# Attention, routing and experts in one kernel on one core: one straight code for every chunk of tokens, each with a rider of up to 32 tokens, in place of four code variants per chunk

## The chip, the cores and the metric

The kernel runs on 1 core of one Trainium2 chip. The metric is the device time of one execution in microseconds (us). Engines are named as in the profile: PE is TensorE (PEld its weight loads), DVE VectorE, ACT ScalarE, POOL GpSimd, SP SyncE.

## The reference

Eight batches of attention between 512 positions and 32 state rows, 8 heads of 64, give 8 x 544 = 4352 rows of 512 numbers. Rows with a positive skip score then go through one of eight experts, chosen by a gate; all others are returned as they are.

```python
def _attn_ref(x, state):                 # x [8,8,512,64], state [8,8,32,64]
    a = softmax(scale * x @ state^T);   xread = a @ state
    a2 = softmax(scale * state @ x^T);  sread = a2 @ x
    return concatenate([xread, sread], axis=2)

def _moe_ref(x, w_skip, w_gate, w1, w2): # x [4352, 512], E = 8, F = 1024
    out = x.copy()
    xc = x[x @ w_skip > 0]
    e_idx, gate_w = argmax and its softmax value of xc @ w_gate
    for e in range(8):
        y[e_idx == e] = gate_w * (relu(xc[e_idx == e] @ w1[e]) @ w2[e])
    out[x @ w_skip > 0] = xc + y
```

(Shortened: the softmax is written out in the original, and the sums are spelled in numpy.)

With the inputs used here the experts 0 to 7 get 544, 0, 0, 32, 544, 1024, 512 and 64 tokens.

## The kernel before

**First phase.** Attention is computed batch by batch and its rows are written to `out` in DRAM. Each batch's rows are scored; the numbers of the rows that an expert has to compute are written into that expert's list `lst` in DRAM by indirect DMAs. When most batches are through, the first full chunk (512 tokens of one expert, chunk 0, here of expert 5) starts beside the rest of it.

**Chunks.** `big(c)` computes one chunk of up to `CB` = 512 tokens of one expert. The numbers of its rows come from `lst` (`lfetch`, `lids`), the rows are gathered from `out` by POOL's indirect DMAs (`zgather`, 16 of 32 rows each), turned and split into a high and a low part (`zsplit`). Weights come in eight pieces of w1 and w2 (`wload`, two DMAs of 256 KB each, issued by SP) and are split by ACT and DVE (`wsplit`). Each product is three matmuls (lines 678 to 680). ACT and DVE make the hidden layer's two halves (L1253, L1254). At the chunk's end DVE adds the result to the rows (L1111) and POOL scatters them back to `out` (L1104). The next chunk's list, rows and weights are fetched while the current chunk computes. Each chunk has a written order per engine (`manual_schedule`), so each engine runs the instructions of a chunk, its own and the next one's loads, in the order in which they stand.

**Riders.** An expert's tokens beyond its full chunks, below 385 of them, are computed in single fp32 matmuls by `rider`, whose steps are strewn between the matmuls of a chunk: four list loads (L1144), the row numbers `rid` (L1151), a gather `rx` (L1153), transposes (L1160), the layers `ph` (L1170) and `yr` (L1183), the sum (L1187) and a scatter. With up to 32 tokens the 128 rows of TensorE hold four quarters of the columns, with up to 64 two halves, with up to 128 one piece. The rider's weights `rw` (4 MB) are loaded in the chunk before it (`rload1`, `rload2`).

**What decides the code.** `chunk_list` computes on DVE, from the counts, a small table `ti`: which chunks and which riders there are, their experts and rows. Each engine reads it into registers (`number`, L285). Chunk c, from 1 to 11, exists four times: with a rider of 32, without one, with one of 128 and with one of 64 (`full`, lines 1291 to 1297). The last chunk that there is, the one behind which no other has to be loaded, runs another set of these four, which stands in the `Else` of the chunk (L1306) behind the code of all later chunks. Riders left when the chunks are through are done in `tails` (L1320).

With these inputs chunk 0 is followed by chunks 1 to 4 (experts 0, 4, 5 and 6). The riders in them are the 32 tokens of expert 0, the 32 of expert 3, the 32 of expert 4 and the 64 of expert 7, this last in chunk 4; `tails` has nothing to do.

Of the kernel before, what the change touches and what calls it, by code (L numbers as in the profile page):

```python
# [32 lines left out]
NBIG = NT // BIGMIN  # L33
NSLOT = 3 * E
# [170 lines left out]
def kernel(ctx, tc, x, state, w_skip, w_gate, w1, w2, out, nb=B):  # L205
# [64 lines left out]
    sizeb = const.tile([P, 3, NSLOT], F32, name="sizeb")  # L270


    ti = const.tile([P, 8], I32, name="ti")
# [16 lines left out]
    def lfetch(c):  # L290

        row = number(c - 1, 5 if c else 1, E * STRIDE - WIN, SP)
        nc.sync.dma_start(out=lis[c % 4][:],
                          in_=lst[ds(row, WIN), :].rearrange("(t p) c -> p t c", p=P))
        size = sizeb[:, 0, c - 1:c] if c else size0[:, 0:1]
# [59 lines left out]
    def expert(c):  # L355
        return number(c - 1, 2 if c else 0, E - 1, SP)
# [133 lines left out]
    thr2 = iota("thr2", [P, E, 3], [[0, E], [P, 3]], 0, 0)  # L490
    slotc = iota("slotc", [P, 1], [[0, 1]], 0, 1)
    slotn = iota("slotn", [P, 1], [[0, 1]], 1, 1)
    stsl = const.tile([P, 3], F32, name="stsl")
    for i, n in enumerate((CB, P, P)):
        G.iota(stsl[:, i:i + 1], pattern=[[0, 1]], base=0, channel_multiplier=n,
               allow_small_or_imprecise_dtypes=True)
    stepn = const.tile([P, 3], F32, name="stepn")
    G.memset(stepn[:], float(P))
    G.memset(stepn[:, 0:1], float(CB))
    cls = const.tile([P, 3], F32, name="cls")  # L500
    for i, n in enumerate((0.0, 32.0, 64.0)):
        G.memset(cls[:, i:i + 1], n)
# [46 lines left out]
    def chunk_list():  # L549
        w = lambda n, s: wk.tile(s, F32, name=n)  # L550
        two = lambda a: a[:].unsqueeze(1).to_broadcast([P, 2, E])
        t8 = w("t8", [P, E, 8])
        nv = w("nv", [P, 3, E])
# [6 lines left out]
        V.tensor_reduce(out=nv[:, 0], in_=t8, axis=AX.X, op=ALU.add)  # L560
        yield
        eb = w("eb", [P, E])
        V.scalar_tensor_tensor(out=eb, in0=nv[:, 0], scalar=float(CB), in1=cw,
# [24 lines left out]
        end = w("end", [P, 1])  # L588
        V.tensor_scalar(out=end, in0=slotn, scalar1=cum[:, 0, E - 1:E], scalar2=4.0,
                        op0=ALU.is_equal, op1=ALU.mult)  # L590
        yield
        ohv = w("ohv", [P, 3, E])
        V.tensor_tensor(out=ohv, in0=ge[:, :, 0:E], in1=ge[:, :, 1:E + 1], op=ALU.subtract)
        yield
        V.tensor_tensor(out=par[:, 2, 0], in0=eb, in1=eu, op=ALU.add)
        yield
        V.tensor_tensor(out=par[:, 2, 1:3], in0=two(cw), in1=two(eu), op=ALU.add)
# [18 lines left out]
        size = w("size", [P, 3])  # L616
# [4 lines left out]
        c3 = w("c3", [P, 3, 3])  # L621
        V.tensor_tensor(out=c3, in0=size[:].unsqueeze(2).to_broadcast([P, 3, 3]),
                        in1=cls[:].unsqueeze(1).to_broadcast([P, 3, 3]), op=ALU.is_gt)
        yield
        kc = w("kc", [P, 3])
        V.tensor_reduce(out=kc, in_=c3, axis=AX.X, op=ALU.add)
        yield
        V.scalar_tensor_tensor(out=kc[:, 0:1], in0=kc[:, 1:2], scalar=1.0, in1=tv[:, 3, 0:1],
                               op0=ALU.add, op1=ALU.mult)
        yield  # L630
        V.tensor_tensor(out=ti[:, 0:1], in0=kc[:, 0:1], in1=end, op=ALU.add)
        yield
        V.tensor_copy(ti[:, 1:2], kc[:, 2:3])
        yield
        V.tensor_copy(ti[:, 2:8].rearrange("p (k a) -> p k a", k=2), tv[:, 0:2, :])
        yield
        dg = w("dg", [P, 3, NSLOT])
        V.tensor_tensor(out=dg, in0=ident[:, 0:NSLOT].unsqueeze(1).to_broadcast([P, 3, NSLOT]),
                        in1=size[:].unsqueeze(2).to_broadcast([P, 3, NSLOT]), op=ALU.mult)
        yield 6  # L640
        psz = ps["t"]([P, 3 * NSLOT], "psz")
        T.matmul(psz, ones[:], dg[:], start=True, stop=True)
        yield 1
        V.tensor_copy(sizeb[:].rearrange("p a n -> p (a n)"), psz)
        yield

    def rest():
# [22 lines left out]
        for f in range(8):  # L670
# [3 lines left out]
            if f == 5:  # L674
                rload(rexpert(0))
# [440 lines left out]
    def rexpert(r, tail=False):  # L1116
        return number(r, 4 if tail else 3, E - 1, SP)
# [18 lines left out]
    def rider(M, r, tail=False):  # L1136
# [4 lines left out]
        row = number(r, 7 if tail else 6, E * STRIDE - P, SP)  # L1141
# [4 lines left out]
        V.tensor_scalar(out=ov, in0=tok[M], scalar1=sizeb[:, 2 if tail else 1, r:r + 1],  # L1146
# [44 lines left out]
    def big(c, M=None, more=True):  # L1191

        xH, xL = xHs[c % 2], xLs[c % 2]
        ride = rider(M, c - 1) if M else iter(())
# [20 lines left out]
        else:  # L1215
# [66 lines left out]
    def kind(c):  # L1282
        return number(c - 1, 0, 8, mybir.ALL_ENGINES)

    def full(c, kd, more):

        def variant(M=None):
            with tc.manual_schedule(engines=order):
                big(c, M, more)

        with tc.If(kd < 3) as cmp2:
            with tc.If(kd > 1) as cmp3:
                variant(32)
            with cmp3.Else():
                variant()
        with cmp2.Else():
            with tc.If(kd > 3) as cmp3:  # L1297
                variant(P)
            with cmp3.Else():
                variant(64)  # L1300

    def chunk(c, kd):
        if c == NBIG:
            full(c, kd - 4, False)
            return
        with tc.If(kd < 5) as cmp:  # L1306
# [6 lines left out]
    def tail_class(r):  # L1313
        return number(r, 1, 3, mybir.ALL_ENGINES) if r < NSLOT else None

    def tails(r, kd):

        if r == NSLOT:
            return
        with tc.If(kd > 0):  # L1320
            kn = tail_class(r + 1)
            if r:
                rload(rexpert(r, tail=True))
            with tc.If(kd > 1) as cmp:
                with tc.If(kd > 2) as cmp2:
                    for _ in rider(P, r, tail=True):
                        pass
                with cmp2.Else():
                    for _ in rider(64, r, tail=True):
                        pass  # L1330
            with cmp.Else():
                for _ in rider(32, r, tail=True):
                    pass
            tails(r + 1, kn)
# [5 lines left out]
    kt = tail_class(0)  # L1340
    kd = kind(1)
    with tc.If(kd > 0):
        chunk(1, kd)
    tails(0, kt)
# [25 lines left out]
```

## Time and profile before

| | us |
|---|---|
| runs | 424.32, 427.35, 429.0 |
| median | 427.35 |
| the profiled execution | 421.62 |
| its span in the trace | 419.3 |
| PE busy | 355.9 (85% of the span) |
| PE idle ahead of a chunk's first matmul (L678, `ph`) | 29.3, of which 28.2 put down to `issue` |
| chunks 1 to 4 on PE | 172.81 to 406.08 |

Times inside the trace count from the span's start. `issue` is time in which an engine waited for nothing that the profile shows. A row's `COMPARE_BRANCH` is the instruction of an engine's sequencer that decides on a jump; these are not counted as busy.

### The profile page before, as it was taken

The page shows a single profiled execution, that of the slowest core. Times are in us where ns is not written, and L with a number is a line of the kernel's source. Part 1 is how long each engine was busy: PE and PEld are TensorE (multiplying, and loading weights), DVE is VectorE, ACT ScalarE, POOL GpSimd, SP SyncE. Part 2 cuts the span into 40 slices and gives each one's busy share as a digit, 9 for nine tenths or more (in the row PEclk, how much of TensorE's full clock was granted, in tenths as well). Part 3 has the DMA queues.
Part 4 walks back from the last instruction along what each step waited for, and adds up shares of the span by engine and source line. Part 5 has one row for each costly group of instructions (what it writes and reads, how often), then busy time and mean ns, then how long its engine had stood idle before and what let it go on. Part 6 is the DMA issues. An engine that isn't in the chain of part 4 may idle for free. (4 is left out here: it accounts for less than half of the span.)

```text
span 419.3 us, 7772 instructions
## 1 busy us (share of the span) xinstructions
PE 355.9 (85%) x2675; PEld 281.0 (67%) x2675; DVE 224.8 (54%) x437; ACT 153.8 (37%) x279; POOL 195.4 (47%) x232
## 2 busy tenths in 40 slices
PE   7699897988789959999996999969999405999960
PEld 7577676876668848887784877758878304876750
DVE  1599998999768623644464435463364700433130
ACT  3589775775562223223231232313233200232000
POOL 8357497687385460427713377231774400310030
PEclk9789997989899988999998999989999955999995
DMA  7916975865694069975598443994539930125621
GB/s 223 182 27 171 303 206 166 214 128 175 193 352 126 1 131 356 389 233 152 167 315 293 111 152 114 367 369 115 146 103 302 370 115 8 42 72 202 213 84 35
DMA packets 77075, 77.81 MB, mean 186 GB/s; under 512 B 30608, under 2 KB 59280, under 8 KB 75952
## 3 DMA queue, kind: packets, MB, share of 16 engines
q1 hardware_dynamic: 70320, 62.25, 48.8%
q0 software_dynamic: 6112, 14.32, 10.6%
q8 instruction: 36, 0.59, 0.7%
q14 instruction: 63, 0.52, 0.5%
q10 hardware_dynamic: 544, 0.13, 0.1%
HBM read 60.95 MB, written 14.83 MB: 181 GB/s over the span
## 5 line engine op out<-in xcount | busy, mean ns | idle before, releaser
L678 PE MATMUL ph<-xH,wH 128*128 128x512 f32 x160 | 68.0, 425 | 29.3 <-issue 28.2
L1253 ACT ACTIVATE hH<-ph 128x512 fp32r<-128x512 f32 x40 | 23.9, 598 | 139.6 <-PE ph L680 135.9
L1254 DVE SCALAR_TENSOR_TENSOR hL<-ph,hH 128x512 fp32r<-128x512 f32 x40 | 27.6, 691 | 72.0 <-ACT hH L1253 72.0
L680 PE MATMUL ph<-xH,wL 128*128 128x512 f32 x160 | 65.2, 407 | 0.5 <-DVE wL L382 0.5
L679 PE MATMUL ph<-xL,wH 128*128 128x512 f32 x160 | 65.3, 408 | 0.0
L678 PE MATMUL y<-wH,hH 128*128 128x512 f32 x160 | 63.5, 397 | 0.0
L679 PE MATMUL y<-wL,hH 128*128 128x512 f32 x160 | 62.6, 391 | 0.0
L680 PE MATMUL y<-wH,hL 128*128 128x512 f32 x160 | 62.6, 391 | 0.0
L678 PEld LDWEIGHTS ph<-xH,wH 128*128 128x128 f32 x160 | 31.8, 199 | 38.4 <-issue 30.3
L343 POOL DMA_INDIRECT z<-out_dram,zi x48 | 50.2, 1045 | 14.6 <-issue 14.6
L382 DVE TENSOR_TENSOR wL<-raw,wH 128x1024 fp32r<-128x1024 f32 x40 | 48.9, 1223 | 8.4 <-ACT wH L379 8.1
L411 POOL DMA_INDIRECT lst<-pays,si x34 | 36.0, 1058 | 19.1 <-issue 7.2
L379 ACT CAST wH<-raw 128x1024 fp32r<-128x1024 f32 x40 | 41.7, 1042 | 6.5 <-PE y L680 4.2
L1104 POOL DMA_INDIRECT out_dram<-xg,sid x20 | 20.8, 1038 | 36.0 <-DVE xg L1111 32.4
L680 PEld LDWEIGHTS ph<-xH,wL 128*128 128x128 f32 x160 | 31.6, 198 | 8.4 <-DVE wL L382 1.0
L678 PEld LDWEIGHTS y<-wH,hH 128*128 128x128 f32 x160 | 30.1, 188 | 9.2 <-issue 3.0
L679 PEld LDWEIGHTS ph<-xL,wH 128*128 128x128 f32 x160 | 31.9, 199 | 6.2
L680 PEld LDWEIGHTS y<-wH,hL 128*128 128x128 f32 x160 | 30.0, 188 | 6.6
L679 PEld LDWEIGHTS y<-wL,hH 128*128 128x128 f32 x160 | 30.1, 188 | 6.2
L1153 POOL DMA_INDIRECT rx<-out_dram,rid x4 | 5.0, 1244 | 55.2 <-DVE rid L1151 36.3
L318 POOL DMA_INDIRECT xg<-out_dram,sid x20 | 20.9, 1046 | 13.8 <-issue 11.3
L1104 POOL DMA_INDIRECT out_dram<-rx,rid x4 | 4.8, 1188 | 48.1 <-DVE rx L1187 25.7
(195 smaller groups left out, 604.5 us busy)
## 6 DMA issues: line engine op xcount, KB each, us to landing
raw<-in_moe_w_dram SPq DMA_DIRECT2D x80, 256.0 KB
rw<-in_moe_w_dram SPq DMA_DIRECT2D x40, 512.0 KB
out_dram<-xr SPq DMA_DIRECT2D x8, 1024.0 KB
xt<-in_x_dram SPq DMA_DIRECT2D x6, 1024.0 KB
xt<-in_x_dram SPq DMA_DIRECT2D x4, 256.0 KB
xt<-in_x_dram SPq DMA_DIRECT2D x2, 512.0 KB
z<-out_dram,zi POOLq DMA_INDIRECT x48, 3.0
sd<-in_state_dram SPq DMA_DIRECT2D x10, 64.0 KB
```

Source lines behind the costliest of these rows:

```text
L318: G.indirect_dma_start(xgs[c % 2][:, t, :], None, out[0:rows, :], bass.IndirectOffsetOnAxis(ap=sis[c % 4][:, t:t + 1], axis=0), bounds_che ...
L343: G.indirect_dma_start(z[:, g], None, rows, bass.IndirectOffsetOnAxis(ap=zis[c % 2][:, g:g + 1], axis=0), bounds_check=4 * NT - 1, oob_is_ ...
L379: A.copy(h, raw)
L382: V.tensor_tensor(out=l, in0=raw, in1=h[:].bitcast(F32), op=ALU.subtract)
L411: d = G.indirect_dma_start(lst[:], bass.IndirectOffsetOnAxis(ap=si[:, j:j + 1], axis=0), pay[:, j, :], None, bounds_check=E * STRIDE - 1, ...
L678: T.matmul(ps, lh, rh, start=first, stop=False)
L679: T.matmul(ps, lh, rl, start=False, stop=False)
L680: T.matmul(ps, ll, rh, start=False, stop=last)
L1104: d = G.indirect_dma_start(rows, bass.IndirectOffsetOnAxis(ap=ids, axis=0), src, None, bounds_check=rows.shape[0] - 1, oob_is_err=False)
L1153: G.indirect_dma_start(rx[:, 0:n2], None, rows, bass.IndirectOffsetOnAxis(ap=ids[:, 0:1], axis=0), bounds_check=NT * Q - 1, oob_is_err=False)
L1253: A.activation(hH, ph, AF.Relu)
L1254: V.scalar_tensor_tensor(out=hL, in0=ph, scalar=0.0, in1=hH[:].bitcast(F32), op0=ALU.max, op1=ALU.subtract)
```

## The change

The classes of riders become lists of fixed sizes: CHUNKS of 512, SMALLS of up to 32, LARGES of up to 128, and LEFT, the smalls for which there is no chunk. An expert's remainder of up to 64 becomes one or two smalls, a larger one becomes larges. Every chunk c from 1 to 11 now has a single code: it always carries rider c - 1 of the smalls (which may be empty) and always loads the rows and weights of chunk c + 1, also where that chunk doesn't exist. Chunks are nested in plain `If`s without `Else`. Behind them the smalls that are left run alone, the first with the weights that the last chunk loaded, others in a loop; then the larges in a loop.

With these inputs the smalls are expert 0, 3, 4 and two halves of expert 7: five. Chunks 1 to 4 carry one each, one is left, and there are no larges.

```diff
     def rexpert / rider: by list (SMALLS, LARGES, LEFT) instead of by class and tail
...
-    def big(c, M=None, more=True):
+    def big(c):
         xH, xL = xHs[c % 2], xLs[c % 2]
-        ride = rider(M, c - 1) if M else iter(())
+        more = c < NBIG
+        ride = rider(SMALLS, c - 1) if c else iter(())
...
-            if M:
-                add(1, 2, go)
-                for i in range(10):
-                    add(3 + i // 2, 2 + 4 * (i % 2), go)
-            if c < NSLOT:
-                er = rexpert(c)
-                add(5 if M == P else 4, 3, rload1, er)
-                add(6 if M == P else 5, 4, rload2, er)
+            add(1, 2, go)
+            for i in range(10):
+                add(3 + i // 2, 2 + 4 * (i % 2), go)
+            er = rexpert(SMALLS, c)
+            add(4, 3, rload1, er)
+            add(5, 4, rload2, er)
...
-    def full(c, kd, more):
-        def variant(M=None):
-            with tc.manual_schedule(engines=order):
-                big(c, M, more)
-        with tc.If(kd < 3) as cmp2:
-            with tc.If(kd > 1) as cmp3:
-                variant(32)
-            with cmp3.Else():
-                variant()
-        with cmp2.Else():
-            with tc.If(kd > 3) as cmp3:
-                variant(P)
-            with cmp3.Else():
-                variant(64)
     def chunk(c, kd):
-        if c == NBIG:
-            full(c, kd - 4, False)
-            return
-        with tc.If(kd < 5) as cmp:
-            kn = kind(c + 1)
-            full(c, kd, True)
-            chunk(c + 1, kn)
-        with cmp.Else():
-            full(c, kd - 4, False)
+        with tc.If(kd > 0):
+            kn = there(c + 1) if c < NBIG else None
+            with tc.manual_schedule(engines=order):
+                big(c)
+            if c < NBIG:
+                chunk(c + 1, kn)
...
+    def alone(which, r, load=True):
+        if load:
+            rload(rexpert(which, r))
+        for _ in rider(which, r):
+            pass
...
-    with tc.If(kd > 0):
-        chunk(1, kd)
-    tails(0, kt)
+    chunk(1, k1)
+    with tc.If(left > 0):
+        alone(LEFT, 0, load=False)
+        with tc.For_i(1, left, 1) as r:
+            alone(LEFT, r)
+    with tc.If(larges > 0):
+        G.memset(rx[:], 0.0)
+        with tc.For_i(0, larges, 1) as r:
+            alone(LARGES, r)
```

In `chunk_list` the tables grow from three lists to four, the steps for the rider classes go and steps for the two kinds of thresholds and for the tables `sizeb` and `tiT` come (33 steps on DVE instead of 32); at the start POOL fills some more constants.

What stands on PE at the end of chunk 1 before the change, where its variant with a rider of 32 ends and the variant without one follows (line 680 is the last matmul of a chunk, `ph<-xH` the first of the next code):

```order
L678 MATMUL y_2160<-wH_2131,hH 128x512
L679 MATMUL y_2160<-wL_2134,hH 128x512
L680 MATMUL y_2160<-wH_2131,hL 128x512
L1292 UNCONDITIONAL_BRANCH
L678 MATMUL ph<-xH_2139,wH_102 128x512
L679 MATMUL ph<-xL_2140,wH_102 128x512
```

Some 600 rows further on, behind all four variants, stands how chunk 2 is entered:

```order
L1297 UNCONDITIONAL_BRANCH
L285 TENSOR_LOAD ti
L1306 COMPARE_AND_BRANCH
L1291 COMPARE_AND_BRANCH
L1292 COMPARE_AND_BRANCH
L678 MATMUL ph<-xH_123,wH_102 128x512
L679 MATMUL ph<-xL_124,wH_102 128x512
```

After the change, the same place on PE, the end of chunk 1 and the start of chunk 2:

```order
L689 MATMUL y_2166<-wH_2137,hH 128x512
L690 MATMUL y_2166<-wL_2140,hH 128x512
L691 MATMUL y_2166<-wH_2137,hL 128x512
L292 TENSOR_LOAD ti
L1305 COMPARE_AND_BRANCH
L689 MATMUL ph<-xH_123,wH_102 128x512
L690 MATMUL ph<-xL_124,wH_102 128x512
```

The jump at the variant's end and the 600 rows between have gone, and of the three branches ahead of chunk 2 one is left.

At the program's end SP has these rows after the change, behind the code of chunk 11 (the branches of L1305 close the chunks; L1163 loads the list of the rider that is left; L1329 is the loop for further ones):

```order
L1305 UNCONDITIONAL_BRANCH x12
L292 TENSOR_LOAD ti
L1327 COMPARE_AND_BRANCH
L292 TENSOR_LOAD ti
L1163 ISA
L1163 DMA rli<-lst 32x2
L1163 ISA
L1163 DMA rli<-lst 32x2
L1163 ISA
L1163 DMA rli<-lst 32x2
```

And PE has these at the same place:

```order
L1305 UNCONDITIONAL_BRANCH x12
L292 TENSOR_LOAD ti
L1327 COMPARE_AND_BRANCH
L1179 MATMUL pt<-ident,rx 128x128
L1189 MATMUL ph<-rw_2147,rxT 32x256 x16
L1196 MATMUL pt<-ident,rh 128x128 x2
L1202 MATMUL yr<-rw_2148,rhT 32x128 x32
L1329 COMPARE_AND_BRANCH
```

With these inputs PE and SP come here from the end of chunk 4, over the code of chunks 5 to 11, and the rider that rode in chunk 4 as a form of 64 is, for its second half, done here.

More of the change, by code (lines that the diff above doesn't have):

```diff
@@ L33 @@
 NBIG = NT // BIGMIN
+SMALL = 32
+NSMALL = 2 * E
 NSLOT = 3 * E
@@ L269 @@
     size0 = const.tile([P, 1], F32, name="size0")
-    sizeb = const.tile([P, 3, NSLOT], F32, name="sizeb")
-    ti = const.tile([P, 8], I32, name="ti")
+    CHUNKS, SMALLS, LARGES, LEFT = range(4)
+    sizeb = const.tile([P, 8, NSLOT], F32, name="sizeb")
+    tiT = const.tile([1, 4, NSLOT], I32, name="tiT")
+    ti = const.tile([P, 11], I32, name="ti")
+    EXPERT, ROW = 3, 7
     ti0 = const.tile([1, 2], I32, name="ti0")
@@ L355, in expert @@
     def expert(c):
-        return number(c - 1, 2 if c else 0, E - 1, SP)
+        return number(c - 1, EXPERT + CHUNKS if c else 0, E - 1, SP)
     def wload(c, e, f0, f1):
@@ L489 @@
     thr = iota("thr", [P, E, 8], [[0, E], [CB, 8]], BIGMIN, 0)
[L490 removed]
+    thr2 = const.tile([P, 2, E, 3], F32, name="thr2")
+    sgn2 = const.tile([P, 2, E, 3], F32, name="sgn2")
+    G.memset(sgn2[:], 1.0)
+    G.memset(sgn2[:, 0, :, 2], -2.0)
+    for i, n in enumerate((0, SMALL, 2 * SMALL)):
+        G.memset(thr2[:, 0, :, i], float(n))
+    for i, n in enumerate((2 * SMALL, P, 2 * P)):
+        G.memset(thr2[:, 1, :, i], float(n))
     slotc = iota("slotc", [P, 1], [[0, 1]], 0, 1)
[L492 to L494 removed]
+    steps = (CB, SMALL, P, SMALL)
+    stsl = const.tile([P, 4], F32, name="stsl")
+    stepn = const.tile([P, 4], F32, name="stepn")
+    for i, n in enumerate(steps):
         G.iota(stsl[:, i:i + 1], pattern=[[0, 1]], base=0, channel_multiplier=n,
                allow_small_or_imprecise_dtypes=True)
[L497 to L502, printed above, removed]
+        G.memset(stepn[:, i:i + 1], float(n))
     le = const.tile([P, E, E], F32, name="le")
@@ L549, in chunk_list @@
     def chunk_list():
[L550 to L553, printed above, removed]
+        w = lambda n, s, tag=None: wk.tile(s, F32, name=n, **(dict(tag=tag) if tag else {}))
+        many = lambda a, n: a[:].unsqueeze(1).to_broadcast([P, n, E])
+        t8 = w("t8", [P, E, 8], "t64")
+        nv = w("nv", [P, 4, E])
         cw = w("cw", [P, E])
@@ L559, in chunk_list @@
         yield
-        V.tensor_reduce(out=nv[:, 0], in_=t8, axis=AX.X, op=ALU.add)
+        V.tensor_reduce(out=nv[:, CHUNKS], in_=t8, axis=AX.X, op=ALU.add)
         yield
         eb = w("eb", [P, E])
-        V.scalar_tensor_tensor(out=eb, in0=nv[:, 0], scalar=float(CB), in1=cw,
+        V.scalar_tensor_tensor(out=eb, in0=nv[:, CHUNKS], scalar=float(CB), in1=cw,
                                op0=ALU.mult, op1=ALU.min)
@@ L587, in chunk_list @@
         yield
-        end = w("end", [P, 1])
-        V.tensor_scalar(out=end, in0=slotn, scalar1=cum[:, 0, E - 1:E], scalar2=4.0,
-                        op0=ALU.is_equal, op1=ALU.mult)
+        V.tensor_scalar(out=ti[:, LARGES - 1:LEFT], in0=cum[:, LARGES:LEFT + 1, E - 1], scalar1=0.0,
+                        scalar2=None, op0=ALU.max)
         yield
-        ohv = w("ohv", [P, 3, E])
+        ohv = w("ohv", [P, 4, E])
         V.tensor_tensor(out=ohv, in0=ge[:, :, 0:E], in1=ge[:, :, 1:E + 1], op=ALU.subtract)
         yield
-        V.tensor_tensor(out=par[:, 2, 0], in0=eb, in1=eu, op=ALU.add)
+        V.tensor_tensor(out=par[:, 2, CHUNKS], in0=eb, in1=eu, op=ALU.add)
         yield
-        V.tensor_tensor(out=par[:, 2, 1:3], in0=two(cw), in1=two(eu), op=ALU.add)
+        V.tensor_tensor(out=par[:, 2, 1:4], in0=many(cw, 3), in1=many(eu, 3), op=ALU.add)
         yield
@@ L620, in chunk_list @@
         yield
-        c3 = w("c3", [P, 3, 3])
-        V.tensor_tensor(out=c3, in0=size[:].unsqueeze(2).to_broadcast([P, 3, 3]),
-                        in1=cls[:].unsqueeze(1).to_broadcast([P, 3, 3]), op=ALU.is_gt)
+        V.tensor_copy(ti[:, CHUNKS:CHUNKS + 1], tv[:, 3, CHUNKS:CHUNKS + 1])
         yield
-        kc = w("kc", [P, 3])
-        V.tensor_reduce(out=kc, in_=c3, axis=AX.X, op=ALU.add)
+        V.tensor_copy(ti[:, EXPERT:].rearrange("p (k a) -> p k a", k=2), tv[:, 0:2, :])
         yield
-        V.scalar_tensor_tensor(out=kc[:, 0:1], in0=kc[:, 1:2], scalar=1.0, in1=tv[:, 3, 0:1],
-                               op0=ALU.add, op1=ALU.mult)
+        dg = w("dg", [P, 8, NSLOT], "t192")
+        diag = lambda out, a, n: V.tensor_tensor(
+            out=out, in0=ident[:, 0:NSLOT].unsqueeze(1).to_broadcast([P, n, NSLOT]),
+            in1=a.unsqueeze(2).to_broadcast([P, n, NSLOT]), op=ALU.mult)
+        diag(dg[:, 0:4], size[:], 4)
         yield
-        V.tensor_tensor(out=ti[:, 0:1], in0=kc[:, 0:1], in1=end, op=ALU.add)
+        diag(dg[:, 4:6], tv[:, 0, LARGES:LEFT + 1], 2)
         yield
[L633 to L639, printed above, removed]
+        diag(dg[:, 6:8], tv[:, 1, LARGES:LEFT + 1], 2)
         yield 6
-        psz = ps["t"]([P, 3 * NSLOT], "psz")
+        psz = ps["t"]([P, 8 * NSLOT], "psz")
         T.matmul(psz, ones[:], dg[:], start=True, stop=True)
@@ L1113, in finish, with listed, rexpert @@
         scatter(out[:, :], sis[c % 4][:, t:t + 1], xg)
-    def rexpert(r, tail=False):
-        return number(r, 4 if tail else 3, E - 1, SP)
+    def listed(which, r, k, most):
+        if isinstance(r, int):
+            return number(r, (EXPERT, ROW)[k] + which, most, SP)
+        return nc.values_load(tiT[:, 2 * k + which - LARGES, ds(r, 1)], engines=SP, min_val=0,
+                              max_val=most, skip_runtime_bounds_check_because=WHY)
+    def rexpert(which, r):
+        return listed(which, r, 0, E - 1)
     def rload1(e):
@@ L1134, in rload, with rider @@
         rload2(e)
-    def rider(M, r, tail=False):
+    def rider(which, r):
+        M = steps[which]
         Q = P // M
@@ L1140, in rider @@
         rows = out[:, :].rearrange("n (q d) -> (n q) d", q=Q)
-        row = number(r, 7 if tail else 6, E * STRIDE - P, SP)
+        row = listed(which, r, 1, E * STRIDE - P)
         li = small.tile([P, 2], F32, tag="rli", name="rli")
@@ L1145, in rider @@
         ov = small.tile([P, 1], F32, tag="rov", name="rov")
-        V.tensor_scalar(out=ov, in0=tok[M], scalar1=sizeb[:, 2 if tail else 1, r:r + 1],
+        V.tensor_scalar(out=ov, in0=tok[M], scalar1=sizeb[:, which, ds(r, 1)],
                         scalar2=float(4 * OOB), op0=ALU.is_ge, op1=ALU.mult)
@@ L1280, in big, with there, chunk @@
             pass
-    def kind(c):
-        return number(c - 1, 0, 8, mybir.ALL_ENGINES)
-    def full(c, kd, more):
-        def variant(M=None):
-            with tc.manual_schedule(engines=order):
-                big(c, M, more)
-        with tc.If(kd < 3) as cmp2:
-            with tc.If(kd > 1) as cmp3:
-                variant(32)
-            with cmp3.Else():
-                variant()
-        with cmp2.Else():
-            with tc.If(kd > 3) as cmp3:
-                variant(P)
-            with cmp3.Else():
-                variant(64)
-    def chunk(c, kd):
-        if c == NBIG:
-            full(c, kd - 4, False)
-            return
-        with tc.If(kd < 5) as cmp:
-            kn = kind(c + 1)
-            full(c, kd, True)
-            chunk(c + 1, kn)
-        with cmp.Else():
-            full(c, kd - 4, False)
[L1313 to L1334, printed above, removed]
+    def there(c):
+        return number(c - 1, 0, 1, mybir.ALL_ENGINES)
+    def chunk(c, kd):
+        with tc.If(kd > 0):
+            kn = there(c + 1) if c < NBIG else None
+            with tc.manual_schedule(engines=order):
+                big(c)
[6 more added lines that the diff above has]
+            pass
     todo.append(rest())
@@ L1339 @@
     manual.close()
-    kt = tail_class(0)
-    kd = kind(1)
-    with tc.If(kd > 0):
-        chunk(1, kd)
-    tails(0, kt)
+    k1 = there(1)
+    larges = number(0, LARGES - 1, NSLOT, mybir.ALL_ENGINES)
+    left = number(0, LEFT - 1, NSMALL, mybir.ALL_ENGINES)
+    chunk(1, k1)
[7 more added lines that the diff above has]
+            alone(LARGES, r)
 _INS = ["x", "state", "moe_w_skip", "moe_w_gate", "moe_w1", "moe_w2"]
```

51 lines of the change are left out of this document (29 added, 22 removed).

## The prediction

> **What bounds the kernel now.** I cut the end of the profiled execution at the places where TensorE starts and ends a chunk, and read the windows view with the busy time of each engine (the count of its instructions in brackets), the granted TensorE clock, the DMA share and GB/s:
>
> ```profile
> core 0: us, PE busy (x) PEld busy (x) DVE busy (x) ACT busy (x) POOL busy (x), PEclk, DMA share, GB/s
> 172.81:221.48 48.67, 48.67 (x292) 38.44 (x290) 24.76 (x36) 15.58 (x23) 22.95 (x21) 1.00 0.75 240
> 221.48:225.16 3.68, 0.01 (x1) 0.04 (x1) 3.53 (x5) 0.40 (x1) 2.37 (x3) 0.97 1.07 374
> 225.16:275.99 50.83, 50.83 (x291) 39.62 (x291) 23.17 (x34) 15.01 (x22) 24.35 (x24) 0.97 0.62 203
> 275.99:279.60 3.61, 0.01 (x1) 0.03 (x1) 3.57 (x5) 0.41 (x1) 2.25 (x3) 0.99 1.05 367
> 279.60:330.00 50.40, 50.40 (x291) 39.69 (x291) 23.18 (x34) 14.99 (x22) 25.00 (x24) 0.97 0.63 200
> 330.00:350.91 20.91, 0.00 (x1) 0.03 (x1) 3.91 (x7) 0.41 (x1) 4.58 (x5) 0.60 0.47 156
> 350.91:406.08 55.17, 54.78 (x246) 40.75 (x246) 15.44 (x20) 10.46 (x15) 8.56 (x9) 0.97 0.31 107
> 406.08:419.30 13.22, 0.00 (x0) 0.00 (x0) 0.40 (x1) 0.00 (x0) 1.81 (x2) 0.62 0.23 69
> ```
>
> Long rows are chunks 1 to 4, in which TensorE never pauses; short rows are the gaps behind chunks 1, 2 and 3 and the tail of 13.22. Between chunk 0 and chunk 1 there is no gap at all, as the timeline shows (start, duration):
>
> ```profile
> 172.58 0.39 PE L680 MATMUL y<-wH,hL 128*128 128x512 f32 x1
> 172.81 0.39 PE L678 MATMUL ph<-xH,wH 128*128 128x512 f32 x1
> ...
> 225.16 0.77 PE L678 MATMUL ph<-xH,wH 128*128 128x512 f32 x1 [3.68 <-issue]
> ```
>
> So the stretch is bound by TensorE and by whatever holds it at a chunk's edge. The view of waits (us in total, times, longest) gives for that `issue`, nothing that the profile can name:
>
> ```profile
> PE ph L678 <- issue: 28.2, 3, 20.9
> ```
>
> What TensorE's sequencer does there stands in the branch instructions at the edges (duration min/median/max in ns, first and last start):
>
> ```profile
> L1306 PEldq COMPARE_BRANCH  x1: 71/71/71, 169.7 to 169.7; - x1
> ...
> L1292 PEldq COMPARE_BRANCH  x2: 68/3312/6557, 217.5 to 224.9; - x2
> ...
> L1306 PEldq COMPARE_BRANCH  x1: 7835/7835/7835, 333.1 to 333.1; - x1
> ...
> L1291 PEldq COMPARE_BRANCH  x1: 4837/4837/4837, 341.2 to 341.2; - x1
> ```
>
> A branch that falls through takes 0.07 us (into chunk 1, 169.7; 224.9). A taken one takes 4.8 to 7.8. The one at 217.5 ends at 224.06, and 3.9 us of it lie under matmuls still queued; the rest is the gap. Into chunk 4 four are taken one after the other, at lines 1292, 1306, 1291 and 1297, hence 20.91.
>
> **What the change removes.** At the ends of chunks 1, 2, 3 no variant is left to jump over, and chunk 4 is no longer behind in a block of its own; TensorE meets one branch per edge, which falls through as at 169.7. Gaps: 3.68 + 3.61 + 20.91 = **28.2**.
>
> Chunks 2, 3 and 4 begin at half clock:
>
> ```profile
> 225.16:227.20 2.04, 2.04 (x5) 1.67 (x6) 0.00 (x0) 0.00 (x0) 1.67 (x2) 0.50 0.97 339
> ```
>
> That makes 50.83 and 50.40 of chunk 1's 48.67. With no gap the clock stays up: 2.16 + 1.73. Chunk 4 loses its cold start and its rider of 64, becoming chunk 1's form with a rider of 32: 55.17 - 48.67 = 6.50. Together **10.4**. TensorE's last chunk then ends at 172.81 + 4 x 48.67 = 367.5 instead of 406.08.
>
> What covers that: the next chunk's gathers, splits and weights must be in time without the gap. In chunk 1 they were, with DVE at 24.76, POOL at 22.95 and a share of 0.75 after an edge without a gap, so I cost it at nothing. If the cover fails, each edge pays again at most what the queues did in the gap, 3.7 us; three edges, 0 to 11. I take 0, chunk 1 being the same code on the same engines. Chunk 4 newly issues the loads of a chunk 5 that does not exist (eight weight pairs, 16 gathers whose indices are all out of bounds, splits); as in chunk 3 they fit beside TensorE, 23.18 on DVE, 25.00 on POOL.
>
> **What it adds ahead of chunk 1.** One more small DVE step in `chunk_list`, wider tables, some six more fills on POOL at the start. SyncE there waits for something else:
>
> ```profile
> SPq L293 <- DMA lst<-pays,si: 9.5, 2, 7.3
> ```
>
> The list's rows land after the table is made, so nothing to 1 us; I take 0.3. T, the end of chunk 4 on TensorE, is **367.8**.
>
> **What it adds behind.** Five groups of up to 32 tokens for four chunks: expert 7's 64 tokens are two of them, so one rider runs alone after T, with nothing beside it. Its weights are loaded in chunk 4. I walk the chain from T by these rows:
>
> ```profile
> 336.00:338.00 2.00, 0.00 (x0) 0.00 (x0) 0.00 (x0) 0.00 (x0) 0.00 (x0) 0.50 0.98 325
> 338.00:340.00 2.00, 0.00 (x0) 0.00 (x0) 0.00 (x0) 0.00 (x0) 0.00 (x0) 0.50 0.39 112
> ...
> L1306 SPq COMPARE_BRANCH  x1: 50/50/50, 335.2 to 335.2; - x1
> ...
> L1291 SPq ALU_OP  x1: 44/44/44, 341.3 to 341.3; - x1
> L1291 SPq COMPARE_BRANCH  x1: 54/54/54, 341.4 to 341.4; - x1
> ...
> L1297 SPq ALU_OP  x1: 36/36/36, 343.5 to 343.5; - x1
> ...
> 226.63 1.86 SPq L1144 DMA_DIRECT2D rli<-lst  x4
> ...
> 235.83 0.16 DVE L1151 SCALAR_TENSOR_TENSOR rid<-rli,rov 128x1 int32<-128x1 f32 x1
> ...
> 236.90 1.04 POOL L1153 DMA_INDIRECT rx<-out_dram,rid  x1 [9.77 <-DVE rid L1151]
> ...
> rx<-out_dram,rid POOLq DMA_INDIRECT x4, 3.6
> out_dram<-rx,rid POOLq DMA_INDIRECT x4, 7.1
> ...
> L1183 PE MATMUL yr<-rw,rhT 128*32 128x128 f32 x64 | 2.2, 276 | 0.0
> L1170 PE MATMUL ph<-rw,rxT 128*32 128x256 f32 x32 | 1.9, 382 | 0.0
> ...
> L1178 DVE COPY rhT<-pt 128x256 f32<-128x256 f32 x1 | 0.4, 424 | 1.8 <-PE pt L1177 1.8
> L1177 PE MATMUL pt<-ident,rh 128*128 128x128 f32 x2 | 0.4, 274 | 0.0
> L1172 ACT ACTIVATE rh<-ph 128x256 f32<-128x256 f32 x1 | 0.4, 373 | 0.0
> ...
> L1160 PE MATMUL pt<-ident,rx 128*128 128x128 f32 x1 | 0.3, 273 | 0.0
> L1161 ACT COPY rxT<-pt 128x128 f32<-128x128 f32 x1 | 0.3, 266 | 3.3 <-PE pt L1160 3.3
> ...
> DMA to landing us min/median/max: 3.1/3.6/4.1
> ...
> L1320 PEldq COMPARE_BRANCH  x1: 4907/4907/4907, 406.3 to 406.3; - x1
> ...
> L1320 POOLq EVENT_SEMAPHORE  x5: 17/43/43, 415.3 to 415.7; - x5
> ```
>
> - SyncE jumps over seven unused chunks (335.2 to 341.3, 6.1 us, begun near T). In the closing code behind them it waits for every outstanding load, the useless ones included; behind chunk 3 (end 330.0) the queues were full until 338. T+8; bounds 4.9 and 14.1 (jump after the drain).
> - A second jump over the other closing blocks: 2.1 (341.4 to 343.5), bounds 2.0 and 6.1. T+10.1.
> - Four list loads, 1.9 to issue, then the landing: under load 228.49 to 235.83, 7.3; with queues empty I take 2.5, under the 3.1 of the fastest scatter. Bounds 0.5 and 7.3. T+14.5.
> - rid 0.16, 0.9 to POOL's issue, 3.6 to landing. T+19.2.
> - TensorE's ph and yr, 1.9 + 2.2 warm; cold, at the 0.77 against 0.39 of the matmul rows, 8.1. Transposes and copies 0.4 + 0.4 + 0.4 + 0.3 + 0.3 = 1.8, and 0.4 for handing over between engines. Bounds 6.3 and 10.3; I take cold, since TensorE has stood idle for 20 us by then. T+29.5.
> - Sum 0.35, scatter 3.6 (bounds 3.1 and 7.1). T+33.5.
> - The loop's exit waits for the landing on every engine; then a jump over the unused large loop, 4.9 on TensorE, and the closing work, 415.3 to the span's end 419.3, 4.0. T+42.4, of bounds **32 and 61**.
>
> I take **42**: 367.8 + 42 = 409.8, against the span of 419.3 a gain of 9.5. The profiled execution took 421.62 (2.3 around its span) and so would take 412; the runs' median of 427.35 lies 5.7 above it, and I subtract from the median: **418**.
>
> On the second jump: SyncE's 2.1 us is the shorter of its taken jumps. [...]
>
> **Rivals.**
>
> *Short tail, 408.* Jumps overlap the drain, the queues are empty by T+5 and the matmuls run warm: near the lower bound, T+32, 10 us less. For: the engines wait side by side, and after chunk 1 the queues had less to move. Against: the chain has three transfers and three jumps in series. 0.17.
>
> *The edges keep their stalls, 434.* If the gap were not the jump but the operands of the next chunk, the edges stay: three gaps of 3.6 and chunks of 50.6, 367.8 + 3 x (3.6 + 1.9) = 384.3 for T, 16.5 later. Against: no engine is named as releaser, the branch rows fill the gaps, and the edge into chunk 1 had none. 0.06. [...]
>
> *The tail costs more than all that is removed, 437.* One mechanism: the jumps of the tail fetch only after what the engine waits for, so they add in series (14.1 to SyncE's closing code, 6.1 for the second, 4.9 on TensorE before the rider) and the small loads land as under load (7.3, 7.1): T+61, 428.5 of span against 419.3. It decides from 55.7 on (13.2 + 38.2 + 1% of 427). For: each of these prices occurs above. Against: SyncE, POOL and TensorE each come to their jumps early, since nothing of theirs is left in chunk 4. 0.09.
>
> *The chunks without gaps become bound by transfers, 423.* The gaps let the queues run at a share above 1; that work now lies in the next chunk, 3.7 us of it, whose share goes from 0.62 to about 0.70, where chunk 1 bore 0.75. At half the price of 0 to 11, 5.5 us: 423.5. 0.14.
>
> **How the numbers follow.** Forecast (tail 36 to 48): 0.54, 412 to 424. A measurement of this kernel tells about 1%, 4.3 us, from no change: faster is below 423.1, slower above 431.6. Faster: nearly all of the forecast, 0.52, the short tail 0.17, half of the transfers 0.08: 0.77. Slower: 0.06 + 0.09 less a little that ends nearer, 0.12. The rest, 0.11, is the same. The range reaches from 407, a microsecond under the short tail since chunks of one form differ by half of that (50.83 and 50.40), to 428, where the transfers' upper half lies; it leaves out the two slow rivals and the ends of the others, 0.18.
>
> **What would show it.** TensorE without a gap of over 0.5 us from chunk 0 to the end of chunk 4, each chunk 48.5 to 49, clock 1.00; the branch rows at the edges near 0.07. T near 368. Then a rider with TensorE at 0.50, its list load near T+10 and its scatter near T+30. Wrong would make it: a wait named DVE or DMA at a chunk's first matmul (transfers), gaps put to `issue` at the edges (stalls stay), or a list load later than T+20 (serial jumps).

## The result and the profile after

| | before | after |
|---|---|---|
| median of the runs | 425.84 (420.65 to 429.0) | 408.05 (406.77 to 410.73) |
| ratio | | 0.967, interval 0.956 to 0.978 |
| the profiled execution / its span | 421.62 / 419.3 | 410.73 / 409.0 |
| chunk 1's start to TensorE's end of chunk 4 | 233.3 | 195.6 |
| from there to the span's end | 13.2 | 37.6 |

A second set of runs (e2, e5, e6 and e8) gave 0.967 again (interval 0.958 to 0.975; 403.74 against 416.94). Medians here are of all runs, while ratios leave out runs more than 1.5% above the fastest of their kernel. The experiments e1, e3, e4 and e7 ran on a second chip and e9 to e12 on a third, where the kernel before itself took 476 and 470 us. They are compared only with runs of their own group, and their absolute expectations (408, 424, 390) don't apply.

The windows that answer to those of before, chunks 1 to 4 and the tail:

```profile
core 0: us, PE busy (x) PEld busy (x) DVE busy (x) ACT busy (x) POOL busy (x), PEclk, DMA share, GB/s
175.76:224.29 48.53, 48.53 (x292) 38.61 (x291) 24.88 (x36) 15.44 (x23) 22.95 (x21) 1.00 0.75 236
224.29:273.65 49.36, 49.36 (x292) 38.53 (x291) 26.52 (x39) 15.44 (x23) 26.74 (x25) 1.00 0.72 226
273.65:322.19 48.54, 48.54 (x292) 38.59 (x291) 26.83 (x40) 15.44 (x23) 28.91 (x27) 1.00 0.73 235
322.19:371.40 49.21, 49.21 (x292) 38.42 (x290) 26.62 (x39) 15.50 (x23) 27.65 (x27) 1.00 0.68 219
371.40:409.00 37.60, 6.55 (x100) 3.42 (x99) 4.96 (x10) 1.16 (x3) 6.75 (x7) 0.63 0.27 91
```

There is no row between chunks any more, the clock is 1.00 in all four, and DVE and POOL carry more in a chunk than before without being waited for. At an edge the timeline shows the next chunk's first matmul starting 0.22 us after the last one:

```profile
224.07 0.39 PE L691 MATMUL y<-wH,hL 128*128 128x512 f32 x1
224.29 0.40 PE L689 MATMUL ph<-xH,wH 128*128 128x512 f32 x1
```

TensorE's branches at the chunks' edges and the last one, at the loop over the larges (duration min/median/max in ns, first and last start):

```profile
L1305 PEldq COMPARE_BRANCH  x5: 65/65/7027, 172.5 to 368.0; - x5
...
L1331 PEldq COMPARE_BRANCH  x1: 348/348/348, 403.6 to 403.6; - x1
```

Four fall through in 0.065 to 0.092; the fifth, taken at 368.0 over chunks 5 to 11, takes 7.03. The tail, row by row:

```profile
L1305 SPq EVENT_SEMAPHORE  x9: 17/17/17, 376.9 to 381.5; - x9
...
383.20 2.07 SPq L1163 DMA_DIRECT2D rli<-lst  x4
386.60 0.16 DVE L1170 SCALAR_TENSOR_TENSOR rid<-rli,rov 128x1 int32<-128x1 f32 x1 [7.13 <-SPq L1329]
387.59 1.04 POOL L1172 DMA_INDIRECT rx<-out_dram,rid  x1 [10.27 <-DVE rid L1170]
390.30 0.45 PE L1179 MATMUL pt<-ident,rx 128*128 128x128 f32 x1 [18.80 <-DMA rx<-out_dram,rid]
391.10 3.60 PE L1189 MATMUL ph<-rw,rxT 128*32 128x256 f32 x32 [0.35 <-ACT rxT L1180]
396.24 1.96 PE L1202 MATMUL yr<-rw,rhT 128*32 128x128 f32 x64 [0.52 <-DVE rhT L1197]
398.95 1.01 POOL L1115 DMA_INDIRECT out_dram<-rx,rid  x1 [10.32 <-DVEq L1329]
...
L1356 POOLq DRAIN  x3: 40/107/3510, 404.6 to 408.7; - x3
```

SyncE stands in the closing code of the chunks' `If`s (its semaphore rows) until 381.5, and its list loads follow. TensorE waits 18.8 us for the rider's rows; that one wait is half of the tail.

### The profile page after: what moved, and what is told of

The parts are those of the page before. It is cut to its first block, busy times and chain, and to the rows that moved or that the text cites. A ratio compares the mean times of both kernels' runs of the same rounds, so it can differ in the third digit from the quotient of the medians.

```text
span 409.0 us, 8248 instructions
## 1 busy us (share of the span) xinstructions
PE 353.6 (86%) x2819; PEld 279.5 (68%) x2819; DVE 235.8 (58%) x459; ACT 160.1 (39%) x288; POOL 216.0 (53%) x256
## 3 DMA queue, kind: packets, MB, share of 16 engines
q0 software_dynamic: 6656, 14.33, 10.6%
## 4 chain that ended last, share of the span: by engine, by line
PE 51%; DMA 7%; issue 3%; DVE 1%; POOL 1%; ACT 0%; DVEq 0%; POOLq 0%; ACTq 0%
PE ph L689 8%; PE ph L690 8%; PE ph L691 8%; PE y L689 8%; PE y L691 7%; PE y L690 7%; DMA out_dram<-xg,sid 6%; PE yr L1202 2%; PE ph L1189 2%; DMA xg<-out_dram,sid 1%; POOL lst L418 1%; PE pt L339 1%; DVE xg L1122 1%; DVE wL L389 0%; DVE zt L358 0%
## 5 line engine op out<-in xcount | busy, mean ns | idle before, releaser
L350 POOL DMA_INDIRECT z<-out_dram,zi x64 | 68.7, 1073 | 19.5 <-issue 19.2
L689 PE MATMUL ph<-xH,wH 128*128 128x512 f32 x160 | 65.4, 409 | 0.7 <-ACT wH L386 0.7
L691 PE MATMUL ph<-xH,wL 128*128 128x512 f32 x160 | 63.5, 397 | 0.5 <-DVE wL L389 0.5
L690 PE MATMUL ph<-xL,wH 128*128 128x512 f32 x160 | 63.4, 396 | 0.0
L389 DVE TENSOR_TENSOR wL<-raw,wH 128x1024 fp32r<-128x1024 f32 x43 | 52.6, 1224 | 12.0 <-ACT wH L386 11.7
L386 ACT CAST wH<-raw 128x1024 fp32r<-128x1024 f32 x43 | 44.9, 1043 | 9.3 <-DMA raw<-in_moe_w_dram 4.9
L689 PEld LDWEIGHTS ph<-xH,wH 128*128 128x128 f32 x160 | 30.5, 191 | 8.3 <-ACT wH L386 1.1
L691 PEld LDWEIGHTS ph<-xH,wL 128*128 128x128 f32 x160 | 30.4, 190 | 7.9 <-DVE wL L389 1.0
L690 PEld LDWEIGHTS ph<-xL,wH 128*128 128x128 f32 x160 | 30.6, 191 | 6.1
L325 POOL DMA_INDIRECT xg<-out_dram,sid x20 | 20.9, 1047 | 14.8 <-issue 12.8
L772 POOL TENSOR_TENSOR mb<-ss,mb 128x512 f32<-128x512 f32 x16 | 21.5, 1343 | 12.0 <-DVE mb L896 7.4
```

Source lines behind the costliest of these rows:

```text
L325: G.indirect_dma_start(xgs[c % 2][:, t, :], None, out[0:rows, :], bass.IndirectOffsetOnAxis(ap=sis[c % 4][:, t:t + 1], axis=0), bounds_che ...
L350: G.indirect_dma_start(z[:, g], None, rows, bass.IndirectOffsetOnAxis(ap=zis[c % 2][:, g:g + 1], axis=0), bounds_check=4 * NT - 1, oob_is_ ...
L386: A.copy(h, raw)
L389: V.tensor_tensor(out=l, in0=raw, in1=h[:].bitcast(F32), op=ALU.subtract)
L689: T.matmul(ps, lh, rh, start=first, stop=False)
L690: T.matmul(ps, lh, rl, start=False, stop=False)
```

## The experiments

**Were the gaps the taken jumps (e3, e12)?** One thing is put back: the chunk's code stands twice.

```diff
             kn = there(c + 1) if c < NBIG else None
-            with tc.manual_schedule(engines=order):
-                big(c)
+            with tc.If(kd < 2) as cmp:
+                with tc.manual_schedule(engines=order):
+                    big(c)
+            with cmp.Else():                      # never run
+                with tc.manual_schedule(engines=order):
+                    big(c)
```

> After, with one thing put back: each chunk's code stands twice, the second in an Else that is never run, so that at the end of each chunk every engine has to take one jump over a whole chunk's code. Theory J (the gaps were the taken jumps): TensorE stands still for 3.5 to 4 us behind chunks 1, 2 and 3, the next chunk starts at half clock (1.7 to 2.2 us more), 16 us in all: 422 to 427 us. Rival O (the gaps were operands that came late): no gap, within 2 us of after, 406 to 410.

> The kernel with a far jump put back at the end of each chunk once more, beside three that have none. Theory J, from the first run of it (edges of 3.5, 4.9 and 4.0 us): again gaps of 3.5 to 5 us at three edges and a cold start behind each, 14 to 20 us more than after's 403.7 and 408.1, chunks 2 to 4 at 50 to 51 us on TensorE where after has 48.5 to 49.4. Rival O: no gap.

e3: 494.26 us beside 473.34 for the same kernel with short jumps (e4, same group) and 476.27 for before; TensorE stands 3.5, 4.9 and 4.0 us at the ends of chunks 1, 2 and 3. e12: 485.97, 1.033 of before (interval 1.019 to 1.047), beside 468.13 (e9) and 463.93 (e10) without the jump. An edge of e12, TensorE's wait for `issue`, and its branches at two of the edges:

```profile
248.10 0.79 PE L689 MATMUL ph<-xH,wH 128*128 128x512 f32 x1 [4.28 <-issue]
...
PE ph L689 <- issue: 12.9, 5, 4.3
...
L1307 PEldq COMPARE_BRANCH  x4: 68/3423/7284, 239.9 to 316.1; - x4
```

The gap, its `issue` and the slow start behind it (0.79 us for a matmul that takes 0.39) are back with nothing changed but a jump over a second copy of the code. The gaps sum to 12.4 us in e3 and 12.9 in e12. By the runs that count in the ratios, e12 lies 19 us over e10, and e3, which has one such run, 12.6 over e4; theory J had 14 to 20. Its 50 to 51 us for chunks 2 to 4 did not come: they took 64 to 67, as chunks of e4 without the jump took 63 to 65 there, for a reason that a later part of this section shows. The rival that operands were late is out.

**Any taken jump, or a far one (e4)?** The same, with little in the Else:

```diff
+            with cmp.Else():                      # never run
+                pt = ps["t"]([P, 4, P], "pt")
+                T.transpose(pt[:, 0, :], rx[:, 0:P], ident[:])
+                A.copy(rxT[:, 0:1], pt[:, 0:1])
```

> After, with a jump at the end of each chunk over very little code: the Else that is never run holds one transpose on TensorE and one copy on ScalarE. Theory JD (a taken jump is dear because its target is far from what has been fetched): a short jump costs TensorE under 0.5 us, no gap, 407 to 411 us. Theory JT (any taken jump is dear on TensorE): gaps of 3.5 us and a cold start at three edges as with the long jump, 422 to 427.

473.34 us, 1.006 of before (interval 0.999 to 1.013). Branches and an edge:

```profile
L1307 PEldq COMPARE_BRANCH  x5: 68/68/180, 185.7 to 308.3; - x5
...
246.49 0.39 PE L691 MATMUL y<-wH,hL 128*128 128x512 f32 x1
246.72 0.40 PE L689 MATMUL ph<-xH,wH 128*128 128x512 f32 x1
```

A taken short jump costs 0.18 us and no gap, a far one in the same place 7.28 (e12): what counts is whether the target is far. Where between a single transpose and a chunk's code the price rises, none of these runs shows. From one chunk on, no run shows the longer jump dearer: over seven chunks it took TensorE 7.03 (after), 6.37 (e2) and 3.31 (e9), over one 6.49 (e6) and 7.28 (e12).

**What the lone rider costs (e7), left out with its 32 tokens:**

> After without the code for the smalls that are left: the 32 tokens of the second half of expert 7 are not computed. Measures the lone rider by itself. By the prediction's sum for the tail the rider's own chain (list, gather, matmuls, scatter) is 23 us and one short jump 2 us, and what stays is the drain of the queues, the long jump and the closing work: 19 us behind TensorE's end, 384 to 390 us. Rival (queues and jumps are the larger part of the tail, the rider is small): less than 12 us gained, over 396.

455.72 us, 0.973 of before (interval 0.961 to 0.985), where e4, the nearest kernel of the group, is 1.006; 16.5 us less by the runs that count in the ratios. The tail is 15.9:

```profile
437.60:453.50 15.90, 0.03 (x1) 0.00 (x0) 3.61 (x5) 0.43 (x1) 4.04 (x4) 0.61 0.42 146
```

against 34.7 in e4: the rider is 18.8 us of the tail, less than the 25 that the sum had for it, and more than the rival's 12.

**What sets the rider's start (e5, e6, e9, e10).** Edits: `NBIG = 4` (e5), `NBIG = 5` (e6), no weight loads for chunk 5 (e9: `if c == 5: continue` in `wload`), and `NBIG = 4` with chunk 4 still loading for a chunk 5 (e10: `more = c <= NBIG`).

> After, built for four chunks behind chunk 0 instead of eleven: chunk 4 loads nothing for a chunk 5, and no code of later chunks lies between it and the lone rider, whose weights chunk 4 still loads. By the prediction's sum the long jump and the drain (T+8) go, and the list loads of the rider start near T+3 instead of T+11.8: 8 us less, 398 to 402 us. Rival (the rider's list waits for the rider's weights, which are still loaded): 2 to 3 us less, 405.

> After, built for five chunks: chunk 4 still loads rows and weights for a chunk 5 that doesn't exist, but the jump behind it passes the code of one chunk instead of seven. If the length of the jump matters, 3 to 5 us less than after (403 to 405). If the drain of the useless loads sets the start of the rider's list loads, within 2 us of after (406 to 410), and the list loads start near T+11 again.

> After, but chunk 4 issues no weight loads for the chunk 5 that doesn't exist (4 MB less; that chunk would compute with old weights, and never runs here). All jumps stay. Tail from TensorE's end of chunk 4 in after: 37.5 and 39.9 us, the rider's list loads at T+11.8 and T+12. Theory D (the closing code waits for the queues to empty, which takes until T+9 to T+11): list loads 3 to 5 us earlier, at T+7 to T+8, tail 33 to 36. Theory S (two far jumps in series set the start): list loads at T+11 again, tail 37 to 40.

> The opposite half: built for four chunks, so that no code lies between chunk 4 and the lone rider, but chunk 4 does load rows and weights for a chunk 5. The four-chunk kernel without those loads had a tail of 25.9 us. Theory D (drain): the rider's list and gather now wait behind the useless loads and the tail goes to 32 to 36 us. Theory S (jumps): the tail stays at 26 to 28.

With T the end of TensorE's last matmul of chunk 4 (371.51 in after), all in us behind it:

| kernel | far jump | loads for chunk 5 | last big load ends | list loads | rid | rider on TensorE | tail |
|---|---|---|---|---|---|---|---|
| after | yes | yes | 9.3 | 11.7 | 15.1 | 18.8 | 37.5 |
| e2, after again | yes | yes | 9.9 | 12.5 | 15.9 | 19.6 | 39.9 |
| e6 | over one chunk | yes | 8.4 | 10.7 | 13.9 | 17.5 | 36.0 |
| e5 | no | no | before T | before T | 1.7 | 8.4 | 25.8 |
| e4 (other group) | yes | yes | 4.2 | 7.4 | 10.6 | 14.3 | 34.7 |
| e12 (other group) | yes | yes | 4.8 | 10.2 | 13.4 | 17.0 | 34.7 |
| e9 (other group) | yes | no weights | before T | 3.8 | 10.0 | 14.3 | 33.1 |
| e10 (other group) | no | yes | 4.5 | 2.2 | 7.7 | 11.7 | 30.4 |

e5 is 0.940 of before (interval 0.931 to 0.948), after in the same group 0.967: 392.04 against 403.74 us, more than the 8 us expected. With no closing code to pass, SyncE issued the list loads already at T-9.7, and not near T+3. This kernel holds for at most four chunks behind chunk 0. e6 took 405.04, level with after. In e6 SyncE takes its jump early and then stands in the closing code until the loads have landed:

```profile
L1305 SPq EVENT_SEMAPHORE  x9: 17/17/17, 362.7 to 372.4; - x9
```

372.4 is T+9.2, and the list loads follow: the drain (the wait until the loads issued have landed) decides there, as theory D says, and the length of the jump is worth little. In the other groups the loads ended earlier, at T+4 to T+5. But in e9, with the weights gone, the rider is no earlier on TensorE than in e4:

```profile
437.00 2.77 SPq L1165 DMA_DIRECT2D rli<-lst  x4
437.89 0.97 POOL L1117 DMA_INDIRECT out_dram<-xg,sid  x1 [0.30 <-issue]
443.16 0.16 DVE L1172 SCALAR_TENSOR_TENSOR rid<-rli,rov 128x1 int32<-128x1 f32 x1 [4.91 <-DMA out_dram<-xg,sid]
444.90 1.04 POOL L1174 DMA_INDIRECT rx<-out_dram,rid  x1 [6.03 <-issue]
```

The list loads are issued at T+3.8, earlier than either theory had it, and now `rid` waits for chunk 4's own scatters to land, until T+10. With drain and jump both gone (e5) the same scatters hold only the gather, at T+5.8:

```profile
367.97 0.16 DVE L1170 SCALAR_TENSOR_TENSOR rid<-rli,rov 128x1 int32<-128x1 f32 x1 [0.52 <-DVE rov L1167]
372.05 1.04 POOL L1172 DMA_INDIRECT rx<-out_dram,rid  x1 [3.27 <-DMA out_dram<-xg,sid]
```

So the start is the latest of three: the drain (T+9 in after, T+4 to T+5 in the other groups), the far jumps and their closing code, the scatters' landing (T+5 to T+10). Taking away one leaves the next: without the weights e9's tail is only 1.6 us under e4's. With the other out of the way, both halves, the loads (e10 against e5, 4.6 us, across the groups) and the jump (e10 against e4, 4.3 us), are worth about 4. e10's 30.4 lies between what the two theories gave for it. Neither was right alone.

**No rider left (e8): `SMALL = 64`,** four riders of up to 64 for four chunks.

> After with riders of up to 64 tokens in every chunk: four riders for four chunks, none left for the end. Each chunk's rider costs TensorE 3.9 + 3.7 us instead of 2.2 + 1.9 (as the forms of 64 and 32 stood in the first profile of before), 3.5 us more in each of four chunks, 14 in all; the lone rider's chain of some 20 to 25 us goes. 396 to 403 us by this sum. Rival (the lone rider was hidden behind the drain and the closing work): slower than after by 10 us or more, 418.

402.50 us, 0.955 of before (interval 0.944 to 0.966), beside after's 403.74 and 0.967 in the same group: the intervals overlap, and the two are not told apart. The chunks cost what was expected and the tail gives it back. The first of the four chunks and the tail:

```profile
173.41:225.70 52.29, 52.29 (x247) 39.56 (x246) 25.15 (x36) 15.79 (x23) 24.35 (x21) 1.00 0.71 226
384.00:403.40 19.40, 0.04 (x1) 0.00 (x0) 3.59 (x5) 0.44 (x1) 4.04 (x4) 0.60 0.39 137
```

The four chunks take 210.6 us instead of 195.7, the tail 19.4 instead of 37.6 to 39.9: from chunk 1 on, 230.0 against 233.2 and 235.6.

**An early list and gather for the left rider (e11):** both are issued during chunk 0, into tiles of their own.

```diff
             if f == 5:
                 rload(rexpert(SMALLS, 0))
+        yield
+        listleft()
+        yield 3
+        gatherleft()
...
-        alone(LEFT, 0, load=False)
+        for _ in rider(LEFT, 0, early=(lil, idl, rxl)):
+            pass
```

> A version meant to be better: after, with the list of the first left rider and its rows fetched early, during chunk 0, into tiles of their own; at the end only its matmuls and its scatter are left. TensorE stood at the rider's first instruction at T+10.3 in after and waited for the rows until T+18.9: 8 to 9 us less, tail 29 to 31, some 0.98 of after. Rival (the small loads and the gather in chunk 0 delay chunk 1's rows or weights): chunk 1 starts later by 2 us or more, or gaps appear in it, and the gain is halved.

The tail is 30.0, as expected, with TensorE at the rider at T+8.3 instead of T+14.3 (e4):

```profile
449.32 0.45 PE L1193 MATMUL pt<-ident,rxl 128*128 128x128 f32 x1 [8.33 <-PEq L292]
```

The time, 469.76, is 1.007 of before (interval 0.995 to 1.018) and no better than e9 and e10. The rival came true: a gap appears in chunk 1.

```profile
187.13 2.87 SPq L1166 DMA_DIRECT2D lil<-lst  x4
193.48 0.16 DVE L1174 SCALAR_TENSOR_TENSOR idl<-lil,ovl 128x1 int32<-128x1 f32 x1 [12.92 <-DMA lil<-lst]
196.44 0.79 PE L695 MATMUL y<-wH,hL 128*128 128x512 f32 x1 [9.65 <-DVE hL L1309]
```

SyncE issues the early list only at 187.13, behind weight loads; VectorE stands 12.9 us before it, with the next step of the hidden layer (`hL`) behind that, and TensorE loses 9.6 us in chunk 1. That is more than the 4.7 us by which the tail is shorter than e4's. Whether the idea beats after with the list loads placed elsewhere was not tried, and after itself was not in that group.

**The two kernels once more (e1, e2).**

> The kernel before once more, for a second profile. Theory F (the time of the fetch behind a taken jump varies from run to run, and that is why before scattered over 420.7 to 429.0 us and after only over 406.8 to 410.7): the first phase up to TensorE's first matmul of chunk 1 again near 173 to 176 us, and what differs from the first profile stands in the three gaps (28.2 us then) and the tail. Rival P (the first phase scatters): the gaps together again 27 to 29 us, and the difference stands ahead of chunk 1.

> The kernel after once more, for a second profile and its times beside those of the next three. Theory P (the first phase scatters by some us between executions): TensorE's first matmul of chunk 1 not at 175.8 us as in the first profile but 172 to 175, the four chunks again 195.6 us together within 0.5, the tail 38 within 2. Rival (the new table steps cost 3 us): it stands at 175.5 to 176 again.

e2: chunk 1 starts at 168.1 instead of 175.8, the four chunks are 195.7, the tail 39.9. So the table steps cost nothing that shows; over six profiles (before, after, e2, e5, e6, e8) chunk 1 started between 167.5 and 175.8 with the same work ahead of it but for those steps. Theory P holds in kind, though its 172 to 175 was too narrow. e1's gaps came out as before's:

```profile
PE ph L678 <- issue: 27.1, 4, 19.7
```

27.1 against 28.2: the gaps hardly vary between the two profiles, and theory F falls. Of the 53 us that e1's span is longer, 13.5 stand ahead of chunk 1, as rival P had it, but some 41 inside chunks 1 to 3, which neither expected.

**Where the slower groups lose their time.** There the rider of 32 inside a chunk is handed on late: its first layer on TensorE, and ScalarE's next step. First e4, then e2, then the rider of 64 of e1:

```profile
212.85 2.79 PE L1189 MATMUL ph<-rw,rxT 128*32 128x256 f32 x32
223.79 0.38 ACT L1191 ACTIVATE rh<-ph 128x256 f32<-128x256 f32 x1 [8.38 <-remote]
```
```profile
192.15 1.93 PE L1189 MATMUL ph<-rw,rxT 128*32 128x256 f32 x32
194.61 0.38 ACT L1191 ACTIVATE rh<-ph 128x256 f32<-128x256 f32 x1
```
```profile
430.64 3.65 PE L1170 MATMUL ph<-rw,rxT 128*64 128x512 f32 x16
434.34 0.60 ACT L1172 ACTIVATE rh<-ph 128x512 f32<-128x512 f32 x1 [4.12 <-PE ph L1170]
```

8.2 us are lost between the two rows of e4 (ScalarE's waits there sum to 50.1 over its four chunks, the longest 15.7), 0.5 in e2, and none for the rider of 64 in chunk 4 of e1. That is a single rider of 64, in a chunk that loads nothing for a next one. The weight loads alone don't explain the difference: in e9's chunk 4, which issues none, ScalarE still waits 12.8 us for the rider of 32. Chunk 4 of before is 54.8 long in both its profiles, chunk 4 of e4 64.9 instead of 49.3. That is why e4, the kernel nearest to after there, is level with before (1.006): the chunks give 22.6 us (272.8 less 250.2), the tail takes 21.3. The kernel after itself did not run on those chips. What makes the hand-over late was not tried and stays open; the profile names only something remote.

## Why the prediction was right

The time lies at the low end of the range, 10 us under the forecast of 418, and the profiled execution, 410.73, near the 412 that the sum gave for it. That nearness is in part luck: T came at 371.5 instead of 367.8, most of it through a first phase 3 us longer, and the tail was 4.5 us shorter than the 42 of the sum. By the steps:

- **Gaps, 28.2:** gone. That a far jump makes such a gap is shown for gaps like the first two (e3, e12 against e4); the 20.9 ahead of chunk 4 was not rebuilt and rests on its four branch rows (6.35, 7.84, 4.84 and 4.60 us).
- **Chunks at 48.67:** 48.53, 49.36, 48.54, 49.21, together 195.6 against 194.7; the transfers' rival (0 to 11 us) had at most 1 of it, and no matmul waited.
- **The table, 0.3:** not visible beside a scatter of 8 us in the first phase.
- **The tail, 42:** 37.5 and 39.9. The start of the list loads was put at T+10.1 and came at T+11.7, through the drain as said: SyncE's closing code ended at T+10.0, where the sum had T+8. The second jump was rightly taken as short, 1.6 us from there to the list loads where the long price was 6.1. Four terms were too large: the list's landing (2.5; `rid` ran 1.3 behind the last issue), the way from `rid` to the rows (4.7; 3.7), the rider's cold work (10.3; 7.9 from 390.30 to 398.20, since TensorE was warm again by `yr`, with a granted clock of 1.00 behind 0.52 under `ph`: 1.96 where the cold price was 4.3; in e2 it took 3.6; the 0.4 for handing over, an estimate without a row, came as 0.4 over six hand-overs), and the jump over the larges' loop (4.9; **0.35**). The last is the step that failed in its reason: it took the price of before's last jump, over the code of all the tails, for one that passes the code of a single rider; e4 shows that a near target is cheap. The way from the sum over the scatter to the loop's exit took 5.4 instead of 4.0, and POOL's final drain 3.5 instead of the 2.0 before.
- **Subtracting from the median, 427.35:** this is the larger part of the miss. From chunk 1's start on, the profiles give 246.5 before and 233.2 and 235.6 after: 10.9 to 13.3 gained, where the sum had 9.5 (9.8 without the table). The medians differ by 17.8 and 13.2. The rest of the first difference is probably scatter of the first phase, 172.8 in before's profile and anything from 167.5 to 175.8 in others, and no effect of the change; the executions with the longer times left no trace that could show it.
- **Rivals:** the edges kept nothing; the tail's prices did not all add, since the jumps ran while the queues drained: TensorE's ended at T+3.5 and SyncE's at T+5.4, the last loads at T+9.3. But the slower case was not empty: in e4's group the removed work and the tail cancel.

## What to carry to other kernels

Read a gap that no engine explains off the branch rows of the engine's sequencer: in these runs a branch that falls through, or jumps over at most a single rider's code, cost TensorE 0.07 to 0.35 us, a far one 3.3 (e9) to 7.8 (before), of which only what lay under matmuls still queued was hidden (3.9 of 6.6 at before's first edge). One straight code with work that is sometimes useless can beat variants that have to be jumped over, as long as the useless work is not waited for at the end. It did so here where the riders were handed on in time, and not on the two slower chips. At the end its drain, the far jump and the last scatters lie on top of each other, so that removing the drain or the jump alone brought 1.6 and 4.3 us of tail (e9, e10 against e4), and removing both 11.7 (e5 against after, in another group). Price a leftover by its whole chain, 19 us for 32 tokens, before it is split off: riders twice as wide cost the chunks 15 us, saved that rider, and were level. And an early load helps only if nothing in order behind it has to wait: e11 won 4.7 us at the end and lost 9.6 in chunk 1.

## What the runs showed of the hardware that was not expected

A taken jump on TensorE over a single transpose took 0.18 us, over a chunk's code 7.28 in the same place (e4, e12). And on the chips where the kernel before took 476 and 470 instead of 417 us, the fp32 matmuls with 32 rows inside a chunk were handed on late (ScalarE waited up to 15.7 us in e4), while the one rider with 64 rows (ScalarE 0.05 us behind its last matmul, e1) and those that ran alone at the end (0.07, e4) were not late, and the large matmuls' pitch (0.23, e4) was as in after.
